# The last 96 rows of a gMLP weight: one transfer, or seventeen

## The chip, the core and the metric

The kernel runs on one core of a Trainium2 chip. The core has a matrix engine (TensorE, in the profile PE, with its weight loads as PEld), a vector engine (VectorE, DVE), a scalar engine (ScalarE, ACT), GpSimd (POOL), and a queue engine (SyncE, SP) that does nothing here but issue transfers. Sixteen DMA engines move data between the chip's main memory (HBM) and the core's own memory, which has 128 partitions. SP and ACT can both issue transfers. The metric is the device time of one execution in microseconds; several runs are given by their median.

## The reference

Two branches read the same normalised input and are added to it. Batch 4, one token, width D = 640.

```
xn  = layernorm(x)                                   # [4, 1, 640]
q   = xn @ wq                                        # 32 heads of 128
p   = softmax(q . k_cache / sqrt(128))               # 4096 cached keys per head and batch
A   = (p @ v_cache) @ wo                             # [4, 1, 640]
z   = gelu(xn @ w_in)                                # w_in [640, 1728]
z1, z2 = z[:864], layernorm(z[864:])
B   = (z1 * (w_sp * z2 + b_sp)) @ w_out              # w_out [864, 640]
out = x + A + B
```

The two caches are 4 x 32 x 4096 x 128 bf16 each, 134 MB. They are 268 of the 282 MB that the kernel reads; wq and wo have 5.2 MB each, w_in 2.2 MB and w_out 1.1 MB.

## The kernel before, in words

Attention goes in 16 steps `i`, one for each group of eight heads and batch (`divmod(i, 4)`). In a step, K is 128 partitions by 256 positions by 128: 8.4 MB, and so is V. One partition holds 256 consecutive positions of one head. All of it passes through one large tile, `ring`, of five units of 4.2 MB each; a K takes two units and a V half takes one. `ring` also holds wq at the start (two units, `pair(1)`), and the gMLP's w_in and w_out (unit 4, `W_UNIT`) until the gMLP is done.

For a step, DVE multiplies K by the query in four quarters (`product`, line 525) and folds the halves of the 128 (`fold`, line 541); PE sums the rest by matmuls with the identity (`sums`, line 550); DVE, ACT and PE make the softmax; and PE multiplies the probabilities with V (`blocks`, line 623), one step behind K. The gMLP runs inside step 0: `gmlp_in` (line 388) after the third quarter, `gmlp_gelu` after the fourth, then `gmlp_stats` and `gmlp_out` (line 486), which adds its result to the same accumulator `out_ps` that takes the attention's output projection (`group_proj`, line 721).

All large transfers are issued by SP, in the order of the list `loads`: K of step 0 in two halves (line 138), the gMLP's weights (`load_w`), K of step 1, the two V halves of step 0 (line 146), the first output weights (line 157), K of step 2, and so on. `pump` walks the list and calls each load as soon as the units that it writes to have been used by instructions emitted so far; after that the order on SP is fixed, and SP waits in that order for what a transfer needs. Before the list, SP issues wq (line 106). ACT issues x (line 92) and two scalars (lines 110 and 111) at the start, and half of the result at the end; the other half is SP's (line 815). The last output weights come in seven transfers (line 163).

The framework attaches a completion semaphore to each transfer and writes all waits; the kernel names none. The order of PE, DVE, ACT and SP in the main part is the order of the Python calls (`manual_schedule`).

w_out has 864 rows = 6 x 128 + 96. The first 768 rows go in one transfer, six consecutive rows to a partition (line 125). The last 96 rows go one to a partition, into the column block `NFF` = 6 of partitions 0 to 95 (line 129, `FT` = 96). `gmlp_out` reads them with the last two of its fourteen matmuls, on 96 partitions.

Of the kernel before, what the change touches and what calls it, by code (L numbers as in the profile page):

```python
# [20 lines left out]
def kernel(  # L21
# [14 lines left out]
    nc = tc.nc  # L36
    P = nc.NUM_PARTITIONS
# [4 lines left out]
    Fh = F // 2  # L42
# [21 lines left out]
    NFF = Fh // P  # L64
    NFC = NFF + 1
    FT = Fh - NFF * P
    NOH = D // 2
    assert GC * Dh * 4 <= 2048

# [51 lines left out]
    w_out_sb = w_sb[:, DC * F : DC * F + NFC * D].rearrange("p (k n) -> p k n", k=NFC)  # L121

    def load_w():
        nc.sync.dma_start(out=w_in_sb, in_=B_w_in.rearrange("(p c) n -> p c n", c=DC))
        nc.sync.dma_start(
            out=w_out_sb[:, 0:NFF, :],
            in_=B_w_out[0 : NFF * P].rearrange("(p k) n -> p k n", k=NFF),
        )
        nc.sync.dma_start(out=w_out_sb[:FT, NFF, :], in_=B_w_out[NFF * P : Fh])

    k_tiles, v_tiles = {}, {}
    V_CUTS = (0, UC // 2, 3 * UC // 4, 7 * UC // 8, UC)
# [21 lines left out]
    def load_wo(j):  # L154
# [5 lines left out]
        parts += [(hh, 1, slice(0, D)) for hh in range(HT - 4, HT - 1)]  # L160
        parts += [(HT - 1, 1, slice(0, NOH)), (HT - 1, 1, slice(NOH, D))]
        for hh, n, cs in parts:
# [15 lines left out]

    plan_k(0)
    plan("w", W_UNIT, 1, load_w)  # L180
    plan_k(1)
    plan_v(0, 0, V_PAIR)
# [20 lines left out]
    def pump():  # L203
        while loads:
# [29 lines left out]
        out=lane_diag[:],  # L234
        in_=ident_f[:].rearrange("p (h l) -> p l h", h=HT),
# [5 lines left out]
        out=hmask[:],  # L241
        in_=ident_f[:].rearrange("p (h l) -> p h l", h=HT),
# [5 lines left out]
        out=head_scale[:].rearrange("p (h l) -> p h l", h=HT),  # L248
# [11 lines left out]
        out=sel[:],  # L260
        in_=ident_f[:].rearrange("p (g h k) -> p k h g", g=CG, k=GC),
# [5 lines left out]
        out=spread[:],  # L267
        in_=ident[:].rearrange("p (m r) -> p r m", r=HT)[:, :, None, :].to_broadcast(
            [P, HT, HT, LN]
        ),  # L270
# [3 lines left out]
        out=q_lanes[:].rearrange("r b (h l) -> r b h l", h=HT),  # L274
        in_=ident[: HT * Bsz, : HT * Bsz]
# [9 lines left out]
    for g in range(CG):  # L285
        ps = slice(g * QW, (g + 1) * QW)
        for hh in range(QH):
            at_col = (g % 2 * QH + hh) * Bsz
            nc.gpsimd.tensor_copy(
                out=place[ps, hh, at_col : at_col + Bsz], in_=lane_diag[ps, 0:Bsz]  # L290
# [12 lines left out]
    for i in range(NSTAT):  # L303
# [5 lines left out]
        out=rstd[:], in_=mv[:, 1:2], func=ACT.Sqrt, bias=eps_tile[:Bsz], scale=1.0  # L309
# [4 lines left out]
        out=xn_bf[:],  # L314
# [9 lines left out]
    for c in range(DC):  # L324
        nc.tensor.transpose(  # L325
            out=xnT_ps[:, c, :], in_=xn_v[:, c, :], identity=ident[:Bsz, :Bsz]
# [11 lines left out]
    for c in range(DC):  # L338
        for hg in range(NQG):
            g = hg % CG  # L340
            nc.tensor.matmul(  # L341
                out=q_ps[hg // CG][g * QW : (g + 1) * QW, :],
# [7 lines left out]
    used.add("wq")  # L350
    out_ps = ps_out.tile([P, NOH], FP32)
    OG = 32

    def out_sum(half):
        return out_ps[OG * half : OG * half + Bsz, :]

    for half in range(2):
        nc.tensor.matmul(
            out=out_sum(half),
            lhsT=ident[:Bsz, :Bsz],  # L360
            rhs=x_bf[:, half * NOH : (half + 1) * NOH],
            start=True,
# [18 lines left out]
    def gmlp_in():  # L381
        zT = gm["zT"] = ps_pv.tile([P, 2, NFC, Bsz], FP32, tag="pv", name="zT")
        for t in range(2):
            f1 = t * Fh + NFF * P
            w_t = w_in_sb[:, :, t * Fh : f1].rearrange("p c (f k) -> p c k f", k=NFF)
            for k in range(NFC):
                for c in range(DC):
                    nc.tensor.matmul(
                        out=zT[: P if k < NFF else FT, t, k, :],
                        lhsT=w_t[:, c, k, :] if k < NFF else w_in_sb[:, c, f1 : f1 + FT],  # L390
                        rhs=xnT[:, c, 0:Bsz],
# [3 lines left out]
    def gmlp_gelu():  # L395
        zT = gm["zT"]
        zz, gw, gt, z3 = (gm[n] for n in ("zz", "gw", "gt", "z3"))
        nc.vector.tensor_copy(out=zz[:, :, 0:NFF, :], in_=zT[:, :, 0:NFF, :])
        nc.vector.tensor_copy(out=zz[:FT, :, NFF, :], in_=zT[:FT, :, NFF, :])
        nc.vector.tensor_tensor(out=gw[:], in0=zz[:], in1=zz[:], op=ALU.mult)  # L400
# [44 lines left out]
    def gmlp_out():  # L445
# [37 lines left out]
        for k in range(NFC):  # L483
            w = P if k < NFF else FT
            for half in range(2):
                nc.tensor.matmul(
                    out=out_sum(half),
                    lhsT=gm["yT"][:w, k, :],
                    rhs=w_out_sb[:w, k, half * NOH : (half + 1) * NOH],
                    start=False,  # L490
# [226 lines left out]
    def group_proj(hg):  # L717
        o_n = gr.pop(hg)
        for hh in range(HT):
            for half in range(2):  # L720
                nc.tensor.matmul(  # L721
                    out=out_sum(half),
                    lhsT=o_n[:, hh, :],
                    rhs=wo_tiles[hg][:, hh, half * NOH : (half + 1) * NOH],
                    start=False,
# [6 lines left out]
    with tc.manual_schedule(engines={E.PE, E.DVE, E.Activation, E.SP}):  # L732
# [77 lines left out]

        res = work.tile([P, NOH], BF16, name="res")
        out_v = out.flatten_outer_dims()
# [35 lines left out]
```

## Time and profile before

| | |
|---|---|
| median of 3 runs | 662.56 us (662.41 to 662.8) |
| profiled execution, its own time | 664.69 us |
| its span in the profile | 662.9 us |
| DVE busy | 458.5 us (69%) |
| PE busy | 325.6 us (49%) |
| ACT busy | 82.6 us (12%) |
| read from HBM | 282.24 MB, 426 GB/s over the span |
| mean granted TensorE clock | 0.727 |

Times inside the profile count from the start of the span. "Busy" of an engine is the time in which it has an instruction running; issuing a transfer is not counted as busy. The queue of SP is called q1 in the profile, that of ACT q10. A "wait" is the time that an engine stood still before an instruction, put down to what came last of the things that the instruction waited for. "Issue to landing" of a transfer runs from the start of its issuing instruction to the arrival of its last byte as its waiters see it. "The chain that ended last" follows the last instruction back, at each step to what released it.

### The profile page before, as it was taken

To read this page: it belongs to the slowest core of one execution; us is meant where nothing else is said; L and a number is where in the kernel's file an instruction comes from. 1 tells how busy PE (TensorE), PEld (TensorE's weight loads), DVE (VectorE), ACT (ScalarE), POOL (GpSimd) and SP (SyncE) were. 2 spreads that over 40 slices of the span, in tenths; PEclk is the share of its full clock that TensorE was granted. 3 is DMA by queue.
4 is the path that set the end of the run, shared out by engine and by line. 5 is a ranking of instruction groups with operands and counts; after the bars stand their busy time and mean duration, and the time that the engine had idled before them with its cause. 6 is when DMAs were issued, how large, how long until landed. Compare 5 with 4: busy or idle time off the path is not lost.

```text
span 662.9 us, 4934 instructions
## 1 busy us (share of the span) xinstructions
PE 325.6 (49%) x2131; PEld 149.9 (23%) x2131; DVE 458.5 (69%) x265; ACT 82.6 (12%) x202; POOL 5.6 (1%) x29
## 2 busy tenths in 40 slices
PE   0356462635546263463526447253563526457746
PEld 0114130212212132131212223121231212213334
DVE  2495975939488594966949397692957949488940
ACT  0103102020200202011020200202020020200200
POOL 2000000000000000000000000000000000000000
PEclk9765685778877677585867877577786857867886
DMA  9999999999999999999999999999999999999997
GB/s 378 437 398 395 423 458 435 443 429 427 428 439 440 423 443 432 404 463 423 439 436 435 428 443 424 431 439 428 435 436 435 435 435 436 416 429 437 423 429 282
DMA packets 8049, 282.56 MB, mean 426 GB/s; under 512 B 880, under 2 KB 2140, under 8 KB 2524
## 3 DMA queue, kind: packets, MB, share of 16 engines
q1 hardware_dynamic: 8008, 282.25, 99.1%
q8 instruction: 16, 0.26, 0.1%
q14 instruction: 5, 0.04, 0.0%
q10 hardware_dynamic: 20, 0.01, 0.0%
HBM read 282.24 MB, written 0.01 MB: 426 GB/s over the span
## 4 chain that ended last, share of the span: by engine, by line
DMA 62%; DVE 26%; PE 11%; issue 0%; ACT 0%; DVEq 0%; ACTq 0%
DMA ring<-in_A_k_cache_dram 57%; DVE ring L525 19%; PE s_ps L550 8%; DVE ring L541 6%; DMA ring<-in_A_v_cache_dram 3%; DMA ring<-in_A_wq_dram 2%; PE q_ps L341 1%; PE pv_acc L623 1%; PE pv L641 0%; PE out_ps L721 0%; DVE s_sb L564 0%; PE pv L653 0%; ACT pv_sb L637 0%; DVE m L573 0%; ACT res L816 0%
## 5 line engine op out<-in xcount | busy, mean ns | idle before, releaser
L550 PE MATMUL s_ps<-ring,ident 128*128 128x512 bf16 x624 | 212.8, 507 | 291.8 <-DVE ring L541 159.8
L525 DVE TENSOR_TENSOR ring<-ring,qbc 128x8192 bf16<-128x8192 bf16 x64 | 281.8, 4418 | 97.9 <-DMA ring<-in_A_k_cache_dram 97.9
L550 PEld LDWEIGHTS <-ident 128*128 128x128 bf16 x624 | 75.8, 122 | 413.2 <-issue 286.1
L541 DVE TENSOR_TENSOR ring<-ring 128x4096 bf16<-128x4096 bf16 x50 | 114.6, 2291 | 1.6
L623 PE MATMUL pv_acc<-ring,pm 128*32 128x512 bf16 x1008 | 68.7, 412 | 7.3 <-DMA ring<-in_A_v_cache_dram 7.3
L564 DVE TENSOR_REDUCE s_sb<-s_ps 128x64 f32<-128x512 f32 x64 | 43.8, 685 | 25.3 <-PE s_ps L550 25.3
L637 ACT COPY pv_sb<-pv_acc 128x512 f32<-128x512 f32 x16 | 9.4, 586 | 397.5 <-PE pv_acc L623 397.5
L598 ACT ACTIVATE pm<-p,hmask 128x256 bf16<-128x256 bf16 x120 | 49.5, 494 | 0.5
L623 PEld LDWEIGHTS <-pm 128*32 128x32 bf16 x1008 | 38.3, 143 | 38.6 <-issue 28.5
L583 DVE TENSOR_REDUCE nb<-max_ps 128x1 f32<-128x16 f32 x16 | 2.8, 174 | 37.0 <-PE max_ps L577 37.0
L641 PE MATMUL pv<-sel,pv_sb 128*128 128x8 f32 x128 | 17.8, 265 | 11.1 <-ACT pv_sb L637 11.1
L641 PEld LDWEIGHTS pv<-sel,pv_sb 128*128 128x128 f32 x128 | 16.3, 199 | 18.3 <-ACT pv_sb L637 18.3
L682 DVE TENSOR_TENSOR o_n<-pv,rden 128x32 bf16<-128x32 f32 x4 | 0.8, 192 | 15.9 <-PE pv L653 15.8
L575 ACT ACTIVATE lay<-lane_diag,m 128x16 f32<-128x16 f32 x16 | 4.9, 309 | 47.6 <-DVE m L573 47.6
L587 ACT ACTIVATE p<-s_sb,nb 128x256 bf16<-128x256 f32 x16 | 8.1, 508 | 19.5 <-DVE nb L583 19.5
L577 PE MATMUL max_ps<-lay,head_scale 128*128 128x16 f32 x32 | 6.3, 272 | 3.7 <-ACT lay L575 3.7
L511 ACT CAST q_rows<-qr_ps 32x128 bf16<-32x128 f32 x4 | 1.0, 256 | 51.8 <-PE qr_ps L503 51.8
L665 POOL TENSOR_TENSOR own_sum<-acc,hmask 128x32 f32<-128x32 f32 x4 | 2.0, 500 | 621.1 <-ACT p L587 621.1
L573 DVE TENSOR_REDUCE m<-s_sb 128x1 f32<-128x256 f32 x16 | 6.7, 420 | 0.5
L341 PE MATMUL q_ps<-ring,xnT 128*32 128x512 bf16 x40 | 4.5, 631 | 3.9 <-DMA ring<-in_A_wq_dram 3.9
L577 PEld LDWEIGHTS max_ps<-lay,head_scale 128*128 128x128 f32 x32 | 5.0, 199 | 5.6 <-ACT lay L575 5.6
L325 PE MATMUL xnT_ps<-ident,xn_bf 4*128 4x4 bf16 x5 | 0.4, 178 | 11.5 <-DVE xn_bf L313 11.5
(90 smaller groups left out, 74.6 us busy)
## 6 DMA issues: line engine op xcount, KB each, us to landing
ring<-in_A_v_cache_dram SPq DMA_DIRECT2D x7, 4096.0 KB, 23.6
ring<-in_A_k_cache_dram SPq DMA_DIRECT2D x2, 4096.0 KB, 29.2
ring<-in_A_wq_dram SPq DMA_DIRECT2D x1, 5120.0 KB
wo<-in_A_wo_dram SPq DMA_DIRECT2D x3, 1280.0 KB, 25.9
ring<-in_B_w_in_dram SPq DMA_DIRECT2D x1, 2160.0 KB, 38.4
ring<-in_A_v_cache_dram SPq DMA_DIRECT2D x1, 2048.0 KB, 20.5
ring<-in_A_v_cache_dram SPq DMA_DIRECT2D x1, 1024.0 KB, 22.2
ring<-in_A_v_cache_dram SPq DMA_DIRECT2D x2, 512.0 KB
```

The lines of the kernel that those rows point to most:

```text
L341: nc.tensor.matmul(out=q_ps[hg // CG][g * QW : (g + 1) * QW, :], lhsT=xnT[:, c, :], rhs=wq_sb[:, c, hg * QH * Dh : (hg + 1) * QH * Dh], st ...
L525: nc.vector.tensor_tensor(out=t, in0=t, in1=qbcs[i // Bsz][:, i % Bsz, None, :].to_broadcast([P, QC, Dh]), op=ALU.mult,)
L541: nc.vector.tensor_tensor(out=t[:, :, 0:HD2], in0=t[:, :, 0:HD2], in1=t[:, :, HD2:Dh], op=ALU.add)
L550: nc.tensor.matmul(out=s[:], lhsT=ident[:], rhs=t[:, :, g * RW : (g + 1) * RW], start=(g == 0), stop=(g == n - 1),)
L564: nc.vector.tensor_reduce(out=scores[i][:, q * QC : (q + 1) * QC], in_=sums_ps.pop((i, q))[:], axis=AX.X, op=ALU.add,)
L573: nc.vector.tensor_reduce(out=m1[:], in_=scores[i][:], axis=AX.X, op=ALU.max)
L577: nc.tensor.matmul(out=ps[:], lhsT=head_scale[:], rhs=d[:], start=True, stop=True)
L587: nc.scalar.activation(out=p[:], in_=scores.pop(i)[:], func=ACT.Exp, bias=nb[:], scale=scale_qk, accum_out=acc[hg % NACC][:, b : b + 1],)
L598: nc.scalar.activation(out=p_m[i % 2][:, :, h, :], in_=probs[i][:].rearrange("p (n c) -> p n c", c=BC), func=ACT.Copy, scale=hmask[:, h : ...
L623: nc.tensor.matmul(out=pv_acc[g * CW : (g + 1) * CW, :], lhsT=pm[:, n, :, :].rearrange("p h (k c) -> p c (h k)", k=GC)[:, c, :], rhs=v_nat ...
L637: nc.scalar.copy(out=pv_sb[:], in_=pv_acc[:])
L641: nc.tensor.matmul(out=pvs[hg][:, :, b], lhsT=pv_sb[:, k * Dh : (k + 1) * Dh], rhs=sel[:, k, :], start=(k == 0), stop=stop and k == GC - 1,)
```

## The change

In `load_w` the transfer of the last 96 rows of w_out is replaced by seventeen. The first brings rows 0 to 31 of the 96 to partitions 0 to 31. The other 64 rows go in sixteen transfers of four rows: number r (32 to 47) brings rows r, r + 16, r + 32 and r + 48 to the partitions of the same numbers. A row has 640 bf16 values, 1280 bytes; a four-row transfer has 5 KB. Source, destination, number of bytes, and all that reads them stay as they were; so does the place in SP's order, between the first 768 rows of w_out and K of step 1.

```diff
@@ -64,6 +64,7 @@
     NFC = NFF + 1
     FT = Fh - NFF * P
+    TW, TN = 32, 4
     NOH = D // 2
@@ -126,7 +127,11 @@
             in_=B_w_out[0 : NFF * P].rearrange("(p k) n -> p k n", k=NFF),
         )
-        nc.sync.dma_start(out=w_out_sb[:FT, NFF, :], in_=B_w_out[NFF * P : Fh])
+        tail = B_w_out[NFF * P : Fh]
+        nc.sync.dma_start(out=w_out_sb[:TW, NFF, :], in_=tail[:TW])
+        step = (FT - TW) // TN
+        for r in range(TW, TW + step):
+            nc.sync.dma_start(out=w_out_sb[r:FT:step, NFF, :], in_=tail[r::step])
```

## The prediction

> **What bounds the kernel now.** I read the page first (busy shares, traffic in 40 slices, queues, the chain that ended last), then the chain in order of time, then SP's queue around line 129: its issues, its waits, and the landing times.
>
> The page: the busy tenths and rates of the DMA engines in 40 slices, the packets of the two queues, and the shares of the chain.
>
> ```profile
> DMA  9999999999999999999999999999999999999997
> ...
> q1 hardware_dynamic: 8008, 282.25, 99.1%
> ...
> q10 hardware_dynamic: 20, 0.01, 0.0%
> HBM read 282.24 MB, written 0.01 MB: 426 GB/s over the span
> ...
> DMA 62%; DVE 26%; PE 11%; issue 0%; ACT 0%; DVEq 0%; ACTq 0%
> ```
>
> Read here that the transfers fill the span from end to end: 282 MB at 426 GB/s are the 662.9 us. Idle time of DVE or PE is cover; idle time of the transfer queue is lost for good, unless something later is waiting on another engine, and nothing is.
>
> The chain, in order of time (start, us, what):
>
> ```profile
> 0.74 15.37 DMA ring<-in_A_wq_dram
> 16.15 4.48 PE q_ps L341 x31
> 20.65 44.95 DMA ring<-in_A_k_cache_dram
> 65.62 4.44 DVE ring L525
> ```
>
> K of the second step is issued at 20.65 us and lands at 65.6. It was not slow for 45 us: it stood in line behind K of step 0 and the gMLP weights. That line is what the change touches.
>
> SP's issues from 0 to 25 us (start, duration):
>
> ```profile
> 0.74 0.40 SPq L106 DMA_DIRECT2D ring<-in_A_wq_dram  x1
> 1.20 0.93 SPq L138 DMA_DIRECT2D ring<-in_A_k_cache_dram  x2
> 2.17 0.79 SPq L124 DMA_DIRECT2D ring<-in_B_w_in_dram  x1
> 3.00 0.47 SPq L125 DMA_DIRECT2D ring<-in_B_w_out_dram  x1
> 3.51 0.51 SPq L129 DMA_DIRECT2D ring<-in_B_w_out_dram  x1
> 20.65 0.33 SPq L138 DMA_DIRECT2D ring<-in_A_k_cache_dram  x1
> ```
>
> The landings of two of them, from issue:
>
> ```profile
> ring<-in_B_w_in_dram SPq DMA_DIRECT2D x1, 2160.0 KB, 38.4
> ...
> ring<-in_B_w_out_dram SPq DMA_DIRECT2D x1, 960.0 KB, 40.4
> ```
>
> So w_in lands at 2.17 + 38.4 = 40.6 us and the first 768 rows of w_out at 43.4. Now SP's own waits (whole span; total, times, longest):
>
> ```profile
> SPq L163 <- DMA ring<-in_A_v_cache_dram: 14.5, 5, 4.6
> ...
> SPq L138 <- DMA ring<-in_A_wq_dram: 12.1, 1, 12.1
> ...
> SPq L815 <- DMA ring<-in_A_v_cache_dram: 0.9, 1, 0.9
> ...
> SPq L146 <- DMA ring<-in_B_w_out_dram: 0.8, 1, 0.8
> ```
>
> The last gives the tail's landing: V of step 0 is issued at 42.53 for 0.33 us, and the next V waits 0.8 us for w_out: all of w_out is in by 43.7. The first and third rows are the ones to learn from. Line 163 loads output weights into their own buffer, and line 815 stores the result; neither touches a byte of V, yet both wait for V transfers to land. Counting transfers of both queues in program order, each waits for the one eight places before it: the program hands out eight completion semaphores in turn, and a transfer isn't issued before the last one on its semaphore has landed. The third to seventh transfer of the last output weights have V transfers eight places ahead: five waits, as listed.
>
> **The change, part by part.** Removed: one transfer of 96 rows (0.51 us of issue at 3.51, in a stretch where SP then waits 12.1 us for wq: worth nothing). Added in its place: one of 32 rows, the same there, and sixteen of four rows of 1280 B. Bytes are the same. Nothing on PE, DVE or ACT is added but waits for more semaphores; three such checks on SP late in the kernel lasted 17 ns each. What reads the tail, line 486, starts at 63.4, so 15 us of cover lie over any landing before that.
>
> Now the turns. In order: 1 x, 2 wq, 3 and 4 the two scalars, 5 and 6 K of step 0, 7 w_in, 8 w_out, 9 the 32 rows. Four-row transfer #1 is the tenth and waits for wq (16.15, where line 341 starts); #2 and #3 wait for the scalars, in by 10.8; #4 for the first K half (25.8, where DVE starts on it); #5 for the second, issued near 1.67 and about 33.8 on its way (the two halves took 29.2 in the mean, the first 24.6): 35.5; #6 for w_in, 40.6; #7 for w_out, 43.4; #8 for the 32 rows, 43.7; #9 to #16 for #1 to #8; and K of step 1, 26th, for #9. All the time until #7, SP may not pass on to K of step 1, which before was in line from 20.65. So at 43.4 the line behind w_out holds only #1 to #6, 5 KB each, and then runs dry.
>
> The gap, step by step. Ten issues, #7 to #16, stand between 43.45 and K. One lasts 0.334 us (the result's four rows on SP, line 815) with 0.05 between issues (0.74 + 0.40 to 1.20; 3.00 + 0.47 to 3.51): 0.38. #8 is due at 43.83, after the 32 rows are in. #9 to #14 wait for transfers that were in line before 43.4: no wait. #15 is due at 46.5 and waits for #7; x, also four rows of 1280 B, was issued at 0.73 and in use at 2.23, 1.5 us, so #7 is in by 45: no wait, nor for #16 and K. K is issued at 43.45 + 10 x 0.38 = 47.25. From issue to the first bytes: wq was issued at 0.74, and the engines are idle to 1.6 and moving by 1.7, so 0.95. Bytes flow again at 48.2; without the change they flow on from 43.7. The gap is **4.5 us**.
>
> Is it covered? V of step 0 follows K in SP's order (42.5 before, 47.7 now, its turn #10 long in). K lands near 70.1 instead of 65.6, and DVE's wait for it grows from 2.2 to 6.7. The second V half hangs on line 486 (issued near 65.5, as before), which leaves it in line in time. Step 2's K is issued 16.7 us after step 1's has landed, 86.8 instead of 82.3; behind step 1's K stand 9.7 MB (two V halves and an output weight), 22 us at 433 GB/s, so the line doesn't run dry there, and everything behind moves by the gap. Sixteen added transfers are two full turns, so all later ones have the semaphore that they had.
>
> Unknown sizes. An issue lies between 0.27 (the result's other half on ACT) and 0.57 (x on ACT): ten with 0.05 give 3.2 to 6.2, gaps of 3.9 to 6.9; I take SP's own row. The engines don't end together: by 43.7 they had moved 43.7 us x 412 GB/s = 18.0 MB where 16.9 MB were in order before K, a lead of 1.1 MB or 2.5 us of traffic. If that lead is lost too, the gap is worth 7.0; it is there again at 65.6 (26.3 MB moved of 25.3), as at 16.15 after a start from nothing (6.1 of 5.2), so it grows back within a load and I count none. The other way, from 43.7 to 65.6 only 380 GB/s flowed against 433 from there to 651: if K alone on idle engines ran at 433, 2.7 us came back, leaving 1.8. Nothing shows why that stretch was slow, so I take no gain.
>
> The profiled execution took 664.69 us, its span 662.9, 1.8 around it; the median of the runs is 662.56, 2.1 under it. The gap is a difference inside the span and is added to the median: 662.56 + 4.5 = **667.1 us**.
>
> **The rivals.** (a) *The second lap waits for landings.* If a four-row load takes longer than eight issues, 3.1 us, #15, #16 and K wait one after another. The first scalar took from 1.33 to 7.73, 6.4 us, in a full line; with that, #15 goes at 49.85 and K at 50.6, the gap is 7.9, the time 670.5. Against it: the line is empty then, and x took 1.5. Chance 0.12.
>
> (b) *The sixteen go one by one.* If rows r, r+16, r+32, r+48 are taken for a block that overlaps the next one's, each waits for the one before. #1 lands with the tail, near 43.8; fourteen steps of 1.5 us bring #16 to 64.8, K to 65.2, a gap of 22.4, 685 us. For it: no transfer of before writes interleaved partitions, so nothing shows how they are ordered; against it: the two halves of the result, lines 815 and 817, share a tile and wait only each for its own. Chance 0.10. The Trainium skill ("DMA: Bandwidth & Descriptors", sections "Anatomy of one DMA" and "Rules for kernel authors") speaks against the change here: it gives a fixed cost of about 2.0 us to a transfer and counts those under 64 KB as mostly overhead. By its 2.0 the fourteen steps would be 28 us and the time an estimated 692; x's 1.5 us in this trace is a lower price, and in my sum the transfers overlap, so only issues count.
>
> (c) *It is hidden: not slower.* If the turns don't bind (more than eight semaphores, or landings known early), SP issues all sixteen from 4.0 to 10.1 us, inside its 12.1 us wait for wq, and K still goes at 20.65: 662.6. It decides if #16 is issued before 16. Against it: the six waits on V above. Chance 0.06, of which 0.02 for a gain by a smoother stretch after 43.7.
>
> **How the numbers follow.** The plain gap has 0.72. Its own range is 664.4 to 669.6. With (a) and both upper sizes (6.9 + 2.5 = 9.4) in part, 665.0 to 671.5 leaves out (b), (c) and some of the edges, about 2 in 10. A measurement of this kernel can tell 0.2%, 1.3 us (the three runs span 0.4). Slower: the plain gap, (a) and (b), 0.94, less 0.01 for gaps under 1.3; same 0.05; faster 0.02.
>
> **What would show it.** Right: SP's four-row issues at 16.15, 25.8, 35.5, 40.6, and ten in a row from 43.4; K at about 47.3; almost no traffic from 44.5 to 48; step 1's first product at about 70; q1 with 8008 + 64 packets (q10's 20 are 4 + 4 for each four-row transfer and 1 + 1 for each scalar, so sixteen by eight, and 48 for the 32 rows, replace 112). Wrong: K still issued at 20.65 (c); four-row issues 1.5 us or more apart after 43.7 (b); a pause before #15 (a); or the shift at 65.6 given back further on.

## The result, and the profile after

The changed kernel takes **670.65 us** in the median (670.27 to 671.39, four runs) against 662.52 us for the kernel before: a ratio of 1.0123, 95% interval 1.0106 to 1.0141, 8.1 us slower. The forecast was 667.1, range 665.0 to 671.5. The direction and the mechanism hold; the size is nearly double what the sum gave.

The profiled execution took 671.39 us with a span of 669.6. Its page, the busy tenths and rates of the DMA engines in 40 slices, and SP's queue:

```profile
DMA  9959999999999999999999999999999999999996
GB/s 374 438 239 401 433 445 438 427 416 431 436 438 438 436 435 428 438 428 435 431 439 435 436 438 431 428 442 432 423 435 428 435 439 436 436 421 423 436 428 276
...
q1 hardware_dynamic: 8072, 282.25, 97.8%
```

One slice, the third, has fallen to 5 tenths and 239 GB/s; elsewhere the engines are as full as before, but for one tenth in the last slice. The packets of q1 are 8008 + 64, as worked out. Where the slice went is in the chain in order of time (start, us, what; SPq is SP issuing):

```profile
3.16 40.03 DMA ring<-in_B_w_out_dram
...
43.21 0.50 SPq L134
43.71 0.04 issue
43.75 0.50 SPq L134
...
48.07 0.50 SPq L134
...
48.69 23.51 DMA ring<-in_A_k_cache_dram
...
72.22 4.44 DVE ring L530
```

Lines have moved down by five: 134 is the four-row transfer, 143 K, 151 V, 393 and 491 the gMLP's matmuls (388 and 486 before), 530 the product. Before the change the chain jumped from K's issue at 20.65 to its landing. Now ten issues stand in it, one every 0.54 us without a pause, from the landing of w_out at 43.2 to K's issue at 48.69. SP's waits from 0 to 70 us say what held the earlier ones, and the first of the ten (total, times, longest):

```profile
SPq L134 <- DMA ring<-in_A_k_cache_dram: 17.0, 2, 9.2
...
SPq L134 <- DMA ring<-in_A_wq_dram: 12.2, 1, 12.2
SPq L134 <- DMA ring<-in_B_w_in_dram: 4.7, 1, 4.7
SPq L134 <- DMA ring<-in_B_w_out_dram: 1.8, 1, 1.8
```

Transfers of gMLP rows wait for wq, for both halves of K, for w_in and w_out: each for the transfer eight places ahead, none for anything it uses. And this is what the DMA engines did meanwhile (stretch, its length, busy time of each engine, granted clock, DMA share, GB/s):

```profile
0.00:43.70 43.70, 12.96 (x71) 5.01 (x72) 22.78 (x26) 4.29 (x6) 3.75 (x25) 0.77 0.92 387
...
43.70:51.00 7.30, 4.14 (x25) 1.89 (x25) 7.27 (x4) 0.00 (x0) 0.00 (x0) 0.50 0.41 142
```

43.7 us at 387 GB/s are 16.9 MB, just what stands in order before K. In the kernel before the same stretch had 412 GB/s, 18.0 MB: there, engines that were done with w_out were already moving K. From 44 to 49 us they move 9 GB/s. And they were almost empty before SP saw w_out land at 43.2 (same columns, the DMA share is the last but one):

```profile
42.00:43.00 1.00, 1.00 (x3) 0.30 (x2) 1.00 (x1) 0.00 (x0) 0.00 (x0) 0.50 0.09 28
43.00:44.00 1.00, 0.17 (x1) 0.00 (x0) 1.00 (x1) 0.00 (x0) 0.00 (x0) 0.50 0.00 0
```

With 1.02 from 40 to 41 us and 0.67 from 41 to 42, the average engine ran out of work near 41.8 us, an estimate from these shares.

### The profile page after: what moved, and what is told of

It reads as the page before. It is cut to its first block, busy times and chain, and to the rows that moved or that the text cites. A ratio compares the mean times of both kernels' runs of the same rounds, so it can differ in the third digit from the quotient of the medians.

```text
span 669.6 us, 4953 instructions
## 1 busy us (share of the span) xinstructions
PE 323.9 (48%) x2131; PEld 149.8 (22%) x2131; DVE 458.4 (68%) x265; ACT 82.5 (12%) x202; POOL 5.7 (1%) x29
## 4 chain that ended last, share of the span: by engine, by line
DMA 64%; DVE 24%; PE 10%; SPq 1%; issue 1%; ACT 0%; DVEq 0%; ACTq 0%
DMA ring<-in_A_k_cache_dram 49%; DVE ring L530 18%; DMA ring<-in_A_v_cache_dram 9%; PE s_ps L555 7%; DMA ring<-in_B_w_out_dram 6%; DVE ring L546 6%; PE pv_acc L628 1%; SPq L134 1%; PE pv L646 0%; PE out_ps L726 0%; DVE s_sb L569 0%; PE pv L658 0%; SPq L143 0%; ACT pv_sb L642 0%; SPq L125 0%
## 5 line engine op out<-in xcount | busy, mean ns | idle before, releaser
L555 PE MATMUL s_ps<-ring,ident 128*128 128x512 bf16 x624 | 208.1, 499 | 301.2 <-DVE ring L546 167.5
L628 PE MATMUL pv_acc<-ring,pm 128*32 128x512 bf16 x1008 | 72.1, 429 | 6.6 <-DMA ring<-in_A_v_cache_dram 6.6
L603 ACT ACTIVATE pm<-p,hmask 128x256 bf16<-128x256 bf16 x120 | 49.5, 494 | 0.5
```

The source lines that it names most:

```text
L555: nc.tensor.matmul(out=s[:], lhsT=ident[:], rhs=t[:, :, g * RW : (g + 1) * RW], start=(g == 0), stop=(g == n - 1),)
L603: nc.scalar.activation(out=p_m[i % 2][:, :, h, :], in_=probs[i][:].rearrange("p (n c) -> p n c", c=BC), func=ACT.Copy, scale=hmask[:, h : ...
L628: nc.tensor.matmul(out=pv_acc[g * CW : (g + 1) * CW, :], lhsT=pm[:, n, :, :].rearrange("p h (k c) -> p c (h k)", k=GC)[:, c, :], rhs=v_nat ...
```

## The experiments

The theory was: K of step 1 is issued late because of the turns at eight semaphores, and the time lost is the time for which the average DMA engine has no work. Rivals: each small transfer has its own price wherever it stands; and, for the size, only the slowest engine's idle time counts. From the changed kernel's own numbers the theory has a rule: K issued at 48.69 cost 8.1, so the loss is K's issue less 40.6. (First bytes come 0.95 us after an issue, as the prediction worked out, so an issue at 40.6 would bring them at 41.55, about when the average engine runs dry.)

**The kernel before, once more.** K landed at 65.6 in its first profile, after a stretch of 380 GB/s that the prediction had found no cause for.

> The kernel before, profiled once more. If the slow stretch of its first profile (380 GB/s from 43.7 to 65.6 us, K landing at 65.6) was of that one execution, K of step 1 lands near 63.5 us here, as in the run with four four-row transfers, and the span is near 660.6 us. If it belongs to the kernel, K lands at 65.6 again and the span is 662.9.

662.22 us, span 660.4. Its chain from 0 to 90 us, and the stretch:

```profile
20.34 43.06 DMA ring<-in_A_k_cache_dram
```

```profile
43.70:65.60 21.90, 13.41 (x118) 7.43 (x118) 17.06 (x28) 5.77 (x12) 0.00 (x0) 0.66 0.99 428
```

K lands at 63.4, and the stretch runs at 428 GB/s like the rest. The slow stretch was of that one execution, whose time of 664.69 was also 2.2 us over the median. What K's landing is to be compared with is 63.4, so the change delays it by 8.8 us, not 6.6.

**Fewer transfers.** `TW, TN = 32, 4` becomes `80, 4`, `72, 4`, `64, 4`: four, six or eight four-row transfers.

```diff
-    TW, TN = 32, 4
+    TW, TN = 80, 4
```

> Four four-row transfers behind one of 80 rows, instead of sixteen behind 32. Theory, turns: step 1's K is then the fourteenth transfer and waits for the sixth, the second half of step 0's K, so it is issued at about 35.6 us, while w_in and w_out are still moving; no gap: 662.5 us, and K lands near 65.6. Rival, own price: each four-row transfer costs its share of the 8.1 us wherever it stands, 0.5 us each: 664.5 us.

> Six four-row transfers behind one of 72 rows. Turns: step 1's K is the sixteenth and waits for the eighth, the first 768 rows of w_out, so it is issued at about 43.25 us. If a core loses time from the moment that the average DMA engine has run out of work (in the changed kernel K went at 48.69 and cost 8.1 us, so 40.6 cost nothing), 662.5 + 2.65 = 665.2 us. If only the slowest engine counts (first bytes 0.95 us after the issue, the line empty at 43.7): 663.0 us. Own price of 0.5 us each: 665.6 us.

> Eight four-row transfers behind one of 64 rows. Turns: two issues, the seventh and eighth, stand between the landing of w_out and step 1's K: K at 43.2 + 2 x 0.54 = 44.3 us. Average engine: 662.5 + 3.7 = 666.2 us. Slowest engine alone: 664.1 us. Own price of 0.5 us each: 666.6 us. Together with the runs of four and six this is a line that starts at a threshold (turns) or at zero transfers (own price).

Measured: four, 662.32 us (ratio 0.9992, interval 0.9982 to 1.0002); six, 665.22 (1.0038, 1.0026 to 1.005); eight, 666.81 (1.0058, 1.0038 to 1.0078). SP's issue of K in the run with four, in the run with six, and in the run with eight (timeline; start, duration):

```profile
35.42 0.35 SPq L143 DMA_DIRECT2D ring<-in_A_k_cache_dram  x1
```

```profile
43.14 0.36 SPq L143 DMA_DIRECT2D ring<-in_A_k_cache_dram  x1
```

```profile
44.31 0.36 SPq L143 DMA_DIRECT2D ring<-in_A_k_cache_dram  x1
```

They stand where the turns put them: at the landing of K's second half, at the landing of w_out, and two issues after that. Four transfers cost nothing, though each spends 0.58 us of SP's time; six cost something (no run has five). An own price would have charged four of them 2 us. Six transfers are the cleanest size: no issue stands between the landing of w_out and K, and still 2.8 us are lost. The slowest engine alone would have given 663.0 and the average engine 665.2, which is what was measured. For eight it was 664.1 and 666.2, and 666.8 was measured. The chain of that run shows how:

```profile
43.14 23.22 DMA ring<-in_A_k_cache_dram
```

Issued into an empty line, K lands 23.2 us later (23.0 with eight, 23.5 with sixteen). In the kernel before it lands some 20 us after w_out is in (43.2 to 43.7, and 63.4). The 3 us between them are about what 0.95 to the first bytes and a lead of 2.5 make. The lead is there again when K lands: 26.3 MB have moved by then in the run with six (66.4 us at 397 GB/s) as in the kernel before (63.4 us at 415), where 25.3 stand in order up to K. So the engines moved the same bytes 3 us later, and the 3 us are time in which they had no work. The runs so far, with two that follow, in one table; "later" is K's landing against 63.4 and the time against the kernel before on the same chip:

| transfers behind the first | K issued | K lands | later | time later |
|---|---|---|---|---|
| none (before) | 20.34 | 63.4 | | |
| 4 of 4 rows | 35.42 | 63.4 | 0.0 | -0.1 |
| 6 of 4 rows | 43.14 | 66.4 | 3.0 | 2.8 |
| 8 of 4 rows | 44.31 | 67.3 | 3.9 | 4.4 |
| 8 of 8 rows | 44.56 | 67.5 | 4.1 | 4.3 |
| 16 of 4 adjacent rows | 46.16 | 69.3 | 5.9 | 6.0 |
| 16 of 4 rows (the change) | 48.69 | 72.2 | 8.8 | 8.1 |

The landings are of one profiled execution each, the times are medians; the change's profiled execution was 0.7 us over its median, as much as 8.8 and 8.1 differ by. The rule of 40.6 gives 0.3 to 0.7 us less than the times of the other rows from six on.

Once K goes after 43 us, a microsecond of its issue is a microsecond of the kernel: 5.3 us of time for 5.55 of issue, from six transfers to sixteen.

**The same transfers from another queue.** The sixteen are issued by GpSimd, after the set-up of the gMLP's tiles.

```diff
+    def load_tail():
+        tail = B_w_out[NFF * P : Fh]
         step = (FT - TW) // TN
         for r in range(TW, TW + step):
-            nc.sync.dma_start(out=w_out_sb[r:FT:step, NFF, :], in_=tail[r::step])
+            nc.gpsimd.dma_start(out=w_out_sb[r:FT:step, NFF, :], in_=tail[r::step])
...
+    load_tail()
```

> The same seventeen transfers, the sixteen four-row ones issued by GpSimd instead of SP, whose transfers take turns at other semaphores. Turns: step 1's K is the tenth of SP and ACT again and goes at 20.65 us; 662.4 us, whatever GpSimd has to wait for, as long as the rows are in before line 486 of the kernel before needs them (63 us). Rival, own price of the small transfers (half a microsecond each, on four of sixteen DMA engines): 670.6 us.

663.28 us, ratio 1.0018 (1.0009 to 1.0027). SP's issue of K, and K in the chain:

```profile
20.68 0.33 SPq L146 DMA_DIRECT2D ring<-in_A_k_cache_dram  x1
```

```profile
20.68 43.04 DMA ring<-in_A_k_cache_dram
```

K goes at 20.68 and lands at 63.7. So 7.3 of the 8.1 us leave with the turns, and the same sixteen transfers, 5 KB each, cost 0.8 (0.6 to 1.8 by the interval). GpSimd issues its last one at 33.7 us, while the line is still full, so this run takes away the queue that they hold up and the empty line together. Where the 0.8 come from isn't settled: K lands 0.3 us late, and the ten runs lie between 662.61 and 665.19.

**Behind K instead of before it.** The list gets an entry of its own for the sixteen, after K of step 1; `load_tail` is as above, but on SP.

```diff
     plan_k(1)
+    plan(("tail",), 0, 0, load_tail)
     plan_v(0, 0, V_PAIR)
```

> The sixteen four-row transfers issued behind step 1's K instead of before it. K goes at 20.65 us and lands at 63.5 us, as before the change. Turns: the eighth of them is then eight places behind K and can't go before K lands; nine issues of 0.54 us later, at 68.4, the first V half goes, into an empty line; by the rule of the other runs (issue less 40.3 where w_out was last, so issue less 60.4 where K is) it costs 8 us: 670.4 us, as if nothing had been moved. Rival, only the place before K is bad and V has time: 662.4 us.

679.25 us, ratio 1.0249 (1.0232 to 1.0266): a loss of 16.8 us, twice what the theory gave, and worse than the change. SP's two issues of V of step 0, from its timeline:

```profile
69.41 0.37 SPq L154 DMA_DIRECT2D ring<-in_A_v_cache_dram  x1
85.64 0.33 SPq L154 DMA_DIRECT2D ring<-in_A_v_cache_dram  x1
```

The first is where the turns were to put it: K landed at 64.5, nine issues of 0.54 follow, V goes at 69.4. The second was near 65 before. The waits from 44 to 90 us, and the DMA rate in the stretch before it:

```profile
PE zT L397 <- DMA ring<-in_B_w_out_dram: 20.9, 1, 20.9
```

```profile
80.20:85.60 5.40, 2.59 (x16) 1.30 (x17) 3.85 (x12) 3.54 (x8) 0.00 (x0) 0.56 0.02 8
```

The gMLP's first matmuls, which read w_in and nothing of w_out, waited 20.9 us for the four-row transfers. PE's work has a fixed order, so the gMLP ended late, unit 4 of the ring came free late, and the line ran dry a second time, at 8 GB/s for 5.4 us. The waits are in the program: line 397 has four semaphore instructions on PE here, as it has (line 393) in the changed kernel, and none (line 388) in the kernel before. So the framework takes these transfers as touching what the matmuls of w_in read; w_in and w_out are columns of one tile, `ring`. Why it does isn't shown; the runs below show what brings it about.

**Rows next to each other, and the two halves of the step.** First both sides adjacent, then only the source 16 apart, then only the partitions. The last two put the 64 rows on other partitions than the gMLP expects, so its part of the result is another; they are read for their issues.

```diff
-        step = (FT - TW) // TN
-        for r in range(TW, TW + step):
-            nc.sync.dma_start(out=w_out_sb[r:FT:step, NFF, :], in_=tail[r::step])
+        for r in range(TW, FT, TN):
+            nc.sync.dma_start(out=w_out_sb[r : r + TN, NFF, :], in_=tail[r : r + TN])
```

The other two, each against the changed kernel:

```diff
+            at = TW + TN * (r - TW)
+            nc.sync.dma_start(out=w_out_sb[at : at + TN, NFF, :], in_=tail[r::step])
```

```diff
+            at = TW + TN * (r - TW)
+            nc.sync.dma_start(out=w_out_sb[r:FT:step, NFF, :], in_=tail[at : at + TN])
```

> Sixteen four-row transfers as in the change, but of four rows next to each other instead of sixteen apart. If the stride makes the issue dear (0.50 us each where four rows of the result took 0.33), the ten issues shrink to 0.38 each, K goes at 47.1 and the time is 669.0 us. If four rows as such cost that, K stays at 48.7 and the time at 670.6 us.

> Sixteen four-row transfers whose source rows are sixteen apart and whose partitions are next to each other; the 64 rows of w_out are permuted by it, so the gMLP's part of the output is another. If the step in the source makes the issue dear, an issue takes 0.50 us, K goes at 48.7 and the time is 670.6 us; if the step over partitions does, an issue takes 0.29 us, K goes at 46.2 and the time is 668.4 us, and line 388 of the kernel before waits for w_in alone.

> The other half: source rows next to each other, partitions sixteen apart; the same 64 rows are permuted. If the step over partitions makes the issue dear, 0.50 us, K at 48.7, 670.6 us; if the step in the source does, 0.29 us, K at 46.2, 668.4 us.

Adjacent: 668.40 us, ratio 1.0083 (1.0066 to 1.01). One execution each for the others: 669.38 with the step in the source, 670.43 with the step over partitions. The issues of the sixteen in those three runs, in this order (shortest, median, longest in ns, first and last start):

```profile
L133 SPq DMA_DIRECT2D ring<-in_B_w_out_dram x16: 248/293/309, 16.0 to 45.7; - x16
```

```profile
L135 SPq DMA_DIRECT2D ring<-in_B_w_out_dram x16: 247/293/309, 16.0 to 45.8; - x16
```

```profile
L135 SPq DMA_DIRECT2D ring<-in_B_w_out_dram x16: 496/496/661, 16.0 to 47.6; - x16
```

The step over partitions alone makes an issue 0.50 us instead of 0.29. A step of 16 rows in main memory costs nothing on SP. The gMLP's first matmuls wait for w_out in the third run, as in the changed kernel; in the first two they don't, and their semaphore instructions are gone. So that wait comes from the step over partitions too. K goes at 46.16, 46.25 and 48.25.

**Eight rows to a transfer.** `TW, TN = 32, 8`: eight transfers, the same 64 rows.

```diff
-    TW, TN = 32, 4
+    TW, TN = 32, 8
```

> Eight transfers of eight rows, eight apart, behind one of 32 rows. Turns: as with eight four-row ones, two issues stand between the landing of w_out and step 1's K. If an issue costs by the transfer (0.50 to 0.58 us), K goes at 44.3 and the time is 666.8 us, as there. If it costs by the row (0.07 us a row more than four adjacent rows), an issue takes 0.8 us or more, K goes near 45.0 and the time is 667.4 us.

666.72 us, ratio 1.0063 (1.0048 to 1.0078). An issue takes 0.56 us, as an issue of four rows does in the run of eight (0.58; the partitions are eight apart in both): the price is by the transfer, not by the row. Half the transfers with the same bytes lose 4.3 us instead of 8.1: two issues instead of ten stand between the landing of w_out and K, and the 2.8 us of the emptied line stay.

## Why the prediction was right, and where its sum was off

*The turns.* Right in each step: #1 goes after wq, the next ones after K's halves and w_in, ten after w_out. That they are the cause is shown from both sides: the same transfers at other semaphores (0.8 us left of 8.1), and fewer of them at these (nothing lost with four, a loss with six, as the eighth place says).

*Ten issues of 0.38 us.* Too cheap: 0.54, 1.4 us more in K's issue, 48.69 for 47.25. I took the row of the result's four rows, 0.334, because it was SP's own; its partitions are adjacent, and adjacent ones take 0.29 here. The step over partitions is what none of the rows I had contained. The upper bound, 0.57, was the better neighbour by accident: it has adjacent partitions too, and was an issue on ACT.

*The lead, which I counted as none.* This is the step that failed. I argued that the engines' lead of 2.5 us grows back within a load, so that only the slowest engine's idle time counts. The run with six transfers contradicts it: 0.5 us by that account, 2.8 measured. The changed kernel's own engines were out of work near 41.8 us, not 43.7. A lead that grows back has to be paid for again. With the lead and the dearer issues the sum would have been 4.5 + 2.5 + 1.4 = 8.4 us, for the 8.1 measured.

*K's landing without the change.* I compared with 65.6, from a stretch that was 2.2 us slow by chance, and could not tell. It hid most of the lead in my check on K's landing: from 70.1 forecast to 72.2 measured is 2.1, but the delay is 8.8 where I had 4.5. These 4.3 are 1.4 from the issues, 2.2 from the landing to compare with, and 0.7 because K took 23.5 us from its issue where my sum left 22.85. As the lead isn't seen in K's first byte but in its landing, the last two are where it shows. DVE's wait for K, forecast to grow from 2.2 to 6.7 us, grows from 0.6 to 8.7.

*A recovery of 2.7 us*, my lower end, had the same slow stretch for its only evidence, and falls with it.

*The range.* The plain gap's own range ended at 669.6, below the 670.65 measured. The stated range reached 671.5 because it was stretched for rival (a), which did not happen, and in part for both upper sizes at once, which is nearer to what did. That the time lies in it is partly luck. The nearest number of all, 670.5, is (a)'s, for a pause that the trace doesn't have: the time alone could not have told the two apart.

*Fifteen microseconds of cover for the rows.* Wrong, without a price here. I named line 486 as the first to need them. The gMLP's first matmuls, line 388 there, wait for them as well, and their first weight load is at 49.5 in the kernel before and 49.8 in the changed one, 1.7 us after the last issue began. The profile puts 0.3 us of PE's standing down to w_out, but the matmuls start 3.4 us after those before them in both kernels, so nothing was lost. How much was left isn't shown; in the run behind K the same wait lasted 20.9 us.

*The rivals.* (a) No pause stands before the fifteenth issue: eight issues last 4.3 us, and landings are sooner. (b) The four-row transfers don't wait for each other, so a step of 1.5 or 2.0 us was never paid (in the section of the Trainium skill that the prediction names, "Anatomy of one DMA" in "DMA: Bandwidth & Descriptors", the 2.0 is fitted to transfers that GpSimd issues; these are SP's). (c) K doesn't go at 20.65. The Trainium skill's rule against small transfers ("DMA: Bandwidth & Descriptors", section "Rules for kernel authors") points the right way, but it isn't the transfers that cost here: four of them, far below its 64 KB, cost nothing, and sixteen cost 8.1 us through the queue that they hold up.

## What to carry to other kernels

Before splitting a transfer, count: where completion semaphores are handed out in turn, eight of them here, a transfer isn't issued before the one eight places ahead has landed, and all that its queue holds behind it waits too. Extra transfers are free as long as that one lands while others are still moving (four here); after that each costs its issue, and letting the line run dry cost 2.8 us besides. Where many small pieces can't be avoided, give them to a queue whose semaphores the large loads don't share (0.8 us here for sixteen); moving them behind the next load cost 16.8 us here, as the queue was held up there instead and the gMLP waited for them as well. And keep partitions adjacent: the issue took 0.29 us instead of 0.50 here, and the matmuls that read w_in no longer waited.

## What was not expected of the hardware

- Issuing a transfer on SP takes 0.50 us where its four partitions are 16 apart and 0.29 where they are adjacent; a step of 16 rows in main memory makes no difference. In the runs with four, six and eight transfers the four partitions are 4, 6 and 8 apart, and an issue takes 0.58, more than with 16; why is open. Eight partitions, eight apart, cost what four do (0.56 and 0.58).
- The loss of an emptied line is more than the time to the first byte. K, 8.4 MB, needs 22.9 to 23.5 us from its issue into an empty line, in seven runs, and some 20 us from the landing of what stood before it in a full one; with no issue in between, the empty line cost 2.8 us.
